# Two recurrent sequence blocks on one core: the same operations, issued in another order

## The chip, the core and the metric

The kernel runs on one core of a Trainium2 chip. Its engines work side by side, each through its own list of instructions in order: TensorE (PE, with its weight loads as PEld), VectorE (DVE), ScalarE (ACT), GpSimd (POOL), and SyncE (SP), which here only issues DMAs. The metric is the device time of one execution in microseconds (us).

## The reference

Two blocks of 2048 steps by 640 channels are computed, and their outputs stand side by side.

```python
# A: complex diagonal recurrence of 640 states, then back to real channels
Bu = einsum("bld,pd->blp", x, B_bar)
h = Lam_bar * h + Bu[:, t]            # for each t of 2048
y = 2 * einsum("blp,dp->bld", hs, C).real + x * Dskip
# B: 4-tap causal convolution of k, times v, then a 2048-long causal convolution, times q
kv = sum_t(shift(k, t) * shift_k[:, t]) * v
out = q * (irfft(rfft(kv) * rfft(ssm_k)) + kv * ssm_D)
```

## The kernel before

All of SBUF is one tile named `arena`, cut into named regions, all of PSUM one tile named `acc` of eight banks, and the only DRAM scratch is `kv_rows`. So the profile's tile names are nearly always `arena` and `acc`, and an operation is known by its line. The program builds 806 operations (`P.add`), each with a function, the cells that it reads and writes, and the engines that may run it. The string `ORDER` then lists every operation with its engine and PSUM bank: `208T0` is operation 208 on TensorE from bank 0, V is VectorE, A ScalarE, G GpSimd, S the SP queue. `emit` (line 122) walks the string and makes each operation wait for those that it depends on, by cells and by banks. The string was searched by a planner that is not in the file. A lower-case `t` is a TensorE operation of `s1` in its narrow form: 32 matmuls on 64x64 quarters of the array (line 874) in place of 16 on 128x64 halves (line 869).

Part A cuts the 2048 steps into 128 segments of 16.
- **Start.** Three parameter loads (line 355) feed one small transpose on TensorE (363), and from it come, on VectorE, ScalarE and GpSimd, tables of powers and angles: `rr` (line 443, the four 640-wide recurrence matrices, needed by line 587), sines for the Fourier steps (g_q 337 and w_q 298 on GpSimd, then the sine on ScalarE, 341 and 303), exponentials (line 375) and `al_s` (line 401, a sine). `warm` (524) runs matmuls on zeros while TensorE has nothing else. `turn_B` (509) transposes the first 128 rows of B, evicted at line 511.
- **Up.** `up2` (matmuls 566, evicted at 583), `up1` and `up0` (566 and 587, evicted at 607 and 632) compute the inputs of each step and fold them pairwise.
- **Coarse scan.** `coarse` joins the 128 segments, in two halves, on VectorE, with a swap of real and imaginary rows on TensorE (658) between; its first product with PSUM is line 661, its scan 666.
- **Down and out.** `down` spreads the states (689 and 691). If VectorE evicts, it adds the old value (709); if ScalarE does (707), TensorE adds it by another matmul (689). `project` multiplies with C: twenty matmuls of 320 columns (739) for each of 16 row sets, evicted at 748 or at 746 with an addition at 754. Row set 13 comes last, in halves (728, 730).

Part B runs in two halves of 320 channels.
- `conv` (833 to 834, with the taps' products at 205 on VectorE or 206 on ScalarE) does the 4-tap convolution for five blocks of 128 channels. k has one buffer, so the load of the next block's k (807) waits for the last tap of the one before. The rows go to `kv_rows` and come back in another layout (850).
- The long convolution is a Fourier transform in two matmul stages, `s1` (869 or 874, evicted at 879) and `s2` (893, evicted at 906), a complex product (917 to 924) and two stages back, `r2` (938, 943) and `r1` (959, with the product with q at 977, 975, 982), then a store (993). The filter goes through `s1` and `s2` as well.

Four tile shapes of the TensorE array are used: 128x128 (warm, swap, down, project), 128x64 (up, wide s1, s2), 64x64 (narrow s1, C's scaling at 556, r1) and 64x128 (r2).

Of the kernel before, what the change touches and what calls it, by code (L numbers as in the profile page):

```python
# [1084 lines left out]
def plain_order(P):  # L1085
# [16 lines left out]


ORDER = (
# [38 lines left out]
)  # L1143


# [68 lines left out]
```

## Time and profile before

| | us |
|---|---|
| median of 3 runs (194.35 to 196.14) | 195.28 |
| the profiled execution | 193.72 |
| its span, first to last instruction | 192.0 |
| TensorE busy | 182.3 |
| VectorE busy | 160.9 |
| ScalarE busy | 143.6 |
| GpSimd busy | 71.4 |

The page gives busy times and the chain of work that ended last; the chain in order of time says which engine the end hung on at each moment. [...]

### The profile page before, as it was taken

The page shows a single profiled execution, that of the slowest core. Times are in us where ns is not written, and L with a number is a line of the kernel's source. Part 1 is how long each engine was busy: PE and PEld are TensorE (multiplying, and loading weights), DVE is VectorE, ACT ScalarE, POOL GpSimd, SP SyncE. Part 2 cuts the span into 40 slices and gives each one's busy share as a digit, 9 for nine tenths or more (in the row PEclk, how much of TensorE's full clock was granted, in tenths as well). Part 3 has the DMA queues.
Part 4 walks back from the last instruction along what each step waited for, and adds up shares of the span by engine and source line. Part 5 has one row for each costly group of instructions (what it writes and reads, how often), then busy time and mean ns, then how long its engine had stood idle before and what let it go on. Part 6 is the DMA issues. An engine that isn't in the chain of part 4 may idle for free.

```text
span 192.0 us, 7688 instructions
## 1 busy us (share of the span) xinstructions
PE 182.3 (95%) x3417; PEld 120.6 (63%) x3417; DVE 160.9 (84%) x228; ACT 143.6 (75%) x178; POOL 71.4 (37%) x58
## 2 busy tenths in 40 slices
PE   5999998989998999988999999999999999999993
PEld 1455554455565765566756756775788777797772
DVE  1809998768989769999899999999988999896822
ACT  2446996999999988999999899976359753395310
POOL 8396999700000000003400279709362040480050
PEclk9999999999999999999999999999999999999999
DMA  4999999899999998959997699203996914646785
GB/s 93 198 194 186 153 172 143 169 155 246 203 203 189 225 201 122 212 97 107 130 158 210 180 136 174 45 3 106 202 220 108 191 48 133 141 156 155 170 197 155
DMA packets 107883, 30.17 MB, mean 157 GB/s; under 512 B 102602, under 2 KB 107210, under 8 KB 107850
## 3 DMA queue, kind: packets, MB, share of 16 engines
q1 hardware_dynamic: 107562, 29.35, 83.6%
q8 instruction: 27, 0.44, 1.0%
q10 hardware_dynamic: 288, 0.33, 0.6%
q14 instruction: 6, 0.05, 0.1%
HBM read 10.99 MB, written 7.86 MB: 98 GB/s over the span
## 4 chain that ended last, share of the span: by engine, by line
PE 60%; ACT 21%; DVE 13%; issue 3%; DMA 1%; SPq 0%; POOL 0%; DVEq 0%; ACTq 0%; POOLq 0%
PE acc L739 20%; PE acc L566 12%; ACT arena L879 7%; PE acc L893 6%; PE acc L938 6%; DVE arena L709 3%; PE acc L959 3%; DVE arena L906 3%; PE acc L587 3%; DVE arena L833 3%; ACT arena L206 2%; ACT arena L906 2%; PE acc L524 2%; ACT arena L341 2%; PE acc L691 2%
## 5 line engine op out<-in xcount | busy, mean ns | idle before, releaser
L566 PE MATMUL acc<-arena 128*64 128x512 bf16 x400 | 47.5, 389 | 1.1 <-ACT arena L607 0.6
L739 PE MATMUL acc<-arena 128*128 128x320 bf16 x300 | 43.0, 300 | 0.1
L906 ACT CAST arena<-acc 128x960 bf16<-128x960 f32 (+1 forms) x36 | 32.3, 923 | 7.6 <-PE acc L893 7.3
L566 PEld LDWEIGHTS <-arena 128*64 128x64 bf16 x400 | 23.4, 108 | 21.6 <-DVE arena L409 1.0
L739 PEld LDWEIGHTS <-arena 128*128 128x128 bf16 x300 | 28.4, 98 | 11.9 <-ACT arena L879 0.2
L879 ACT CAST arena<-acc 128x1024 bf16<-128x1024 f32 x36 | 34.5, 1051 | 0.6 <-PE acc L874 0.6
L893 PE MATMUL acc<-arena 128*64 128x160 bf16 x512 | 23.4, 235 | 1.5 <-ACT arena L906 0.6
L833 POOL TENSOR_TENSOR arena<-arena 128x2048 bf16<-128x2048 bf16 x1 | 4.1, 4064 | 52.3 <-DVE arena L205 52.3
L893 PEld LDWEIGHTS <-arena 128*64 128x64 bf16 x512 | 17.9, 110 | 8.0 <-ACT arena L906 3.7
L833 DVE TENSOR_TENSOR arena<-arena 128x2048 bf16<-128x2048 bf16 x14 | 19.5, 1394 | 1.1 <-ACT arena L206 0.9
L920 POOL TENSOR_TENSOR arena<-arena 128x1280 bf16<-128x1280 bf16 x4 | 10.9, 2730 | 19.0 <-DMA kv_rows<-arena 15.8
L943 ACT CAST arena<-acc 128x1024 bf16<-128x1024 f32 x15 | 14.4, 1022 | 1.4 <-POOL arena L920 0.9
L709 DVE TENSOR_TENSOR arena<-acc,arena 128x1024 bf16<-128x1024 f32 (+1 forms) x13 | 13.9, 1094 | 0.1
L583 DVE CAST arena<-acc 128x1024 bf16<-128x1024 f32 x7 | 8.5, 1217 | 6.3 <-PE acc L566 6.3
L748 DVE TENSOR_TENSOR arena<-acc,arena 128x640 bf16<-128x640 f32 x10 | 8.2, 823 | 6.5 <-PE acc L739 5.5
L205 DVE TENSOR_SCALAR arena<-arena 128x2048 bf16<-128x2048 bf16 (+1 forms) x16 | 11.0, 711 | 3.0 <-DMA arena<-in_B_k_dram 2.9
L922 POOL TENSOR_TENSOR arena<-arena 128x1280 bf16<-128x1280 bf16 x3 | 8.0, 2654 | 14.4 <-DVE arena L920 14.4
L691 PE MATMUL acc<-arena 128*128 128x512 bf16 (+2 forms) x50 | 12.6, 328 | 0.1
L206 ACT ACTIVATE arena<-arena 128x2048 bf16<-128x2048 bf16 (+2 forms) x9 | 10.8, 1207 | 2.1 <-DVE arena L833 1.7
L869 PE MATMUL acc<-arena 128*64 128x128 bf16 x320 | 11.5, 221 | 0.9 <-ACT arena L560 0.4
L975 ACT CAST arena<-acc 128x640 bf16<-128x640 f32 (+1 forms) x7 | 5.4, 808 | 9.0 <-PE acc L959 9.0
L906 DVE CAST arena<-acc 128x960 bf16<-128x960 f32 (+1 forms) x10 | 10.6, 1057 | 1.4 <-ACT arena L906 0.5
(148 smaller groups left out, 320.0 us busy)
## 6 DMA issues: line engine op xcount, KB each, us to landing
out_dram<-arena SPq DMA_DIRECT2D x31, 160.0 KB, 3.1
arena<-in_B_ssm_k_dram SPq DMA_DIRECT2D x8, 320.0 KB, 5.1
kv_rows<-arena SPq DMA_DIRECT2D x5, 512.0 KB, 3.8
arena<-kv_rows SPq DMA_DIRECT2D x16, 160.0 KB, 4.0
arena<-in_A_x_dram SPq DMA_DIRECT2D x16, 160.0 KB, 3.1
arena<-in_B_q_dram SPq DMA_DIRECT2D x8, 320.0 KB, 4.5
arena<-in_A_B_re_dram ACTq DMA_DIRECT2D x1, 160.0 KB, 2.4
arena<-in_A_B_im_dram ACTq DMA_DIRECT2D x1, 160.0 KB
```

What stands on the lines that cost most here:

```text
L206: self.SM = {nc.scalar: lambda out, in_, by: nc.scalar.mul(out, in_, by), nc.vector: vm(nc.vector), nc.gpsimd: vm(nc.gpsimd)}
L566: e.matmul(o[64 * r:64 * r + 64], lhsT=self.BT[j][:, r, d, :], rhs=self.XP[:, d, 2 * q:2 * q + 2], start=(d == 0), stop=(d == 4), skip_gro ...
L691: e.matmul(B[:, o:o + 128 * k], lhsT=c.RR[:, n, j, :], rhs=A[:, j, q:q + k, 0:128], start=not by_pe, stop=True, skip_group_check=True)
L709: e.tensor_tensor(out=o, in0=b, in1=o, op=ALU.add)
L739: e.matmul(B[:, 512 * b:512 * b + 320], lhsT=lh[j], rhs=self.CT[:, j, 320 * b:320 * b + 320], start=(j == 0), stop=(j == 9))
L833: P.add(f"ca{d}_{j}", tt, lambda e: e.tensor_tensor(out=t1, in0=t1, in1=t2, op=ALU.add), outs=[t1], ins=[t1, t2])
L869: e.matmul(B[64 * b:64 * b + 64, 128 * i:128 * i + 128], lhsT=lh[i], rhs=F[:, b, :], start=True, stop=True, tile_position=(0, 64 * b))
L879: P.add(f"e1{what}{hf}_{u}", {PACT: act(1024), PDVE: dve(1024)}, lambda e, B: c.CP[e](out=out, in_=(B.rearrange("p (l n s k) -> p k s l n" ...
L893: e.matmul(B[64 * s:64 * s + 64, 512 * b + 160 * i:512 * b + 160 * i + 160], lhsT=c.W[:, k, 64 * b:64 * b + 64], rhs=self.AS[hf][:, k, 160 ...
L906: c.CP[e](out=out, in_=b.rearrange("p r (k j n) -> p r k j n", k=n, j=4) if nj > 1 else b.rearrange("p r (k x) -> p r k x", k=n))
L938: e.matmul(B[:, 512 * s + 128 * i:512 * s + 128 * i + 128], lhsT=lh[i][s][r], rhs=rh, start=(r == 0), stop=(r == 1), tile_position=(64 * s ...
L943: P.add(f"er2{hf}_{u}", {PACT: act(1024), PDVE: dve(1024)}, lambda e, B: c.CP[e](out=out, in_=B.rearrange("p (s n b) -> p b s n", s=2, n=4 ...
```

## The change

Only the string `ORDER` is replaced. All 806 operations and all buffers stay; their order, some engines, some banks and some of the narrow forms are others.

```diff
 ORDER = (
-    "83V0 58G0 148S0 85S0 0G0 12T6 21G0 30G0 24V0 108G0 119V0 143G0 15G0 16G0 106G0 149G0 17V0 86S0 5T2 8T3 7T6 22V0 84S0 88T7 89V7 "
+    "155A0 154A0 148S0 0G0 10T4 7T5 83V0 13T6 14T0 21G0 23V0 27V0 34G0 84S0 86S0 85S0 40V0 171S0 15G0 46G0 16G0 107G0 43V0 172S0 "
...
```

Counted from the two strings: 14 operations go from ScalarE to VectorE and 14 back, 3 from VectorE to GpSimd and 5 back. The narrow form of `s1` stands 17 times where it stood 20 times. The places where TensorE goes from one tile shape to another are 85 where there were 98.

The first place is ScalarE's start. A table load is not written in the kernel: the compiler puts one wherever a function follows one of the other set. Before, all exponentials (375) stood ahead of all sines:

```order
L370 ACT_TABLE_LOAD
L370 ACTIVATE arena<-arena 128x10
L375 ACTIVATE arena<-arena 128x10
L789 CAST arena<-arena 128x20
L375 ACTIVATE arena<-arena 128x10 x2
L511 COPY arena<-acc 128x640 x2
L375 ACTIVATE arena<-arena 128x10 x2
L583 CAST arena<-acc 128x2x4x128
L401 ACT_TABLE_LOAD
L401 ACTIVATE arena<-arena 128x80
```

In the changed program ScalarE has, after the same start:

```order
L511 COPY arena<-acc 128x640 x2
L280 ACT_TABLE_LOAD
L280 ACTIVATE arena<-arena 128x64
L341 ACTIVATE arena<-arena 128x32x32
L375 ACT_TABLE_LOAD
L375 ACTIVATE arena<-arena 128x10
L243 COPY arena<-arena 128x64
L375 ACTIVATE arena<-arena 128x10
L401 ACT_TABLE_LOAD
L401 ACTIVATE arena<-arena 128x80
L341 ACTIVATE arena<-arena 128x32x32
L460 ACTIVATE arena<-arena 128x1280
```

Two sines (280, 341) moved ahead of the last two exponentials, so the program holds four table loads where it held two, and the first eviction of `up2` (583) on ScalarE comes later.

The second place is VectorE while TensorE does `up2`: its evictions (583), the additions of the first convolution (833), the recurrence tables (443) and a small table for `s1` (281). Before:

```order
L443 TENSOR_TENSOR arena<-arena 128x1280
L263 TENSOR_TENSOR arena<-arena 128x4
L583 CAST arena<-acc 128x2x4x128
L281 TENSOR_TENSOR arena<-arena 128x256
L583 CAST arena<-acc 128x2x4x128
L833 TENSOR_TENSOR arena<-arena 128x2048
L583 CAST arena<-acc 128x2x4x128
L833 TENSOR_TENSOR arena<-arena 128x2048
```

Now:

```order
L281 TENSOR_TENSOR arena<-arena 128x256
L291 CAST arena<-arena 128x2
L292 TENSOR_SCALAR arena<-arena 128x2
L833 TENSOR_TENSOR arena<-arena 128x2048
L409 MEMSET arena 64x1
L583 CAST arena<-acc 128x2x4x128
L418 RECIPROCAL arena<-arena 128x10
L583 CAST arena<-acc 128x2x4x128 x2
L443 TENSOR_TENSOR arena<-arena 128x1280
L833 TENSOR_TENSOR arena<-arena 128x2048
```

Two evictions more and the first recurrence table moved between the first and the second addition of the convolution.

The third place is TensorE after row set 3 of `project`, in `s2` of the second half (893), where `down` (691) stands between its groups. Before:

```order
L893 MATMUL acc<-arena 64x160
L691 LDWEIGHTS arena
L691 MATMUL acc<-arena 128x512
L691 LDWEIGHTS arena
L691 MATMUL acc<-arena 128x512
L893 LDWEIGHTS arena
```

Now the groups of `s2` follow each other, and `down` comes behind them:

```order
L893 MATMUL acc<-arena 64x160
L893 LDWEIGHTS arena
L893 MATMUL acc<-arena 64x160
L691 LDWEIGHTS arena
L691 MATMUL acc<-arena 128x512
```

Two changes of tile shape, into `down` and back, are gone there.

74 rows, old and new, of the table ORDER are left out of this document.

## The prediction, made before the run

> **What bounds the kernel now.** I read the page's busy times first, then the windows of four stages, then the chain in order of time. The page's first part has each engine's busy time, share and instructions:
>
> ```profile
> PE 182.3 (95%) x3417; PEld 120.6 (63%) x3417; DVE 160.9 (84%) x228; ACT 143.6 (75%) x178; POOL 71.4 (37%) x58
> ```
>
> No engine is idle enough for a simple answer. The windows cut the span, from the first `up2` on, where the chain changes engine; columns are length, then busy time of PE, PEld, DVE, ACT and POOL:
>
> ```profile
> 9.66:40.27 30.61, 29.54 (x346) 16.43 (x345) 23.36 (x23) 24.46 (x25) 25.75 (x18) 1.00 1.15 169
> 40.27:68.14 27.87, 27.28 (x529) 16.98 (x529) 22.49 (x32) 26.78 (x38) 0.00 (x0) 1.00 1.08 213
> 68.14:126.14 58.00, 55.23 (x1269) 37.03 (x1267) 55.84 (x65) 55.52 (x67) 16.98 (x5) 1.00 0.86 141
> 126.14:188.94 62.80, 62.62 (x1252) 46.97 (x1248) 53.65 (x68) 33.28 (x40) 22.86 (x12) 1.00 0.64 145
> ```
>
> From 68 to 126 us VectorE (55.84 of 58.00) and ScalarE (55.52) are full; TensorE has 2.77 us without a matmul. From 126 us on TensorE has no gap to speak of (62.62 of 62.80), and that stage sets the end. The chain, start and length of each piece, says the same:
>
> ```profile
> 7.56 2.18 PE acc L524 x10
> 9.73 11.50 PE acc L566 x100
> ...
> 25.55 2.18 DVE arena L833
> 27.75 2.01 ACT arena L206
> 29.79 2.63 DVE arena L833
> 32.44 2.00 ACT arena L206
> ...
> 39.23 1.00 ACT arena L607
> ...
> 123.16 2.37 DVE arena L879 x2
> 125.57 0.64 PE acc L869 x16
> 126.20 2.82 PE acc L739 x20
> ...
> 186.18 2.73 PE acc L728 x20
> ```
>
> It goes through fillers on TensorE to 9.7, `up2` to 21, then the first convolution, back and forth between VectorE (833) and ScalarE (206), to ScalarE's eviction of `up1` (607) at 40.2; it leaves VectorE's evictions at 125.5 and stays with TensorE up to the last row set's halves (728). So I price the change in four stages, to 40.27, to 68.14, to 126.14 and to the end.
>
> **Changes of tile shape.** Twelve `s2` matmuls alone, twenty-four in a row, twenty matmuls of `project` alone and forty in a row, from the same chain:
>
> ```profile
> 92.07 0.95 PE acc L893 x24
> ...
> 147.06 0.54 PE acc L893 x12
> ...
> 157.32 2.82 PE acc L739 x20
> ...
> 160.99 5.54 PE acc L739 x40
> ```
>
> Two groups apart take 2 x 0.54 = 1.08 against 0.95, and 5.64 against 5.54: a change of shape costs 0.10 to 0.13 us of TensorE. I take 0.10. Of the 13 changes that go, ten lie between the first swap (68.14) and row set 3 (126.14), three behind it, none before. The ten lie where VectorE and ScalarE are full, and count for 0 to -1.0. The three behind it count in full: **-0.3 us**. Three `s1` fewer are narrow; a narrow group and a wide one take
>
> ```profile
> 46.34 0.38 PE acc L874 x32
> 46.71 0.57 PE acc L869 x16
> ```
>
> so that costs at most 3 x 0.19 = 0.57 us of TensorE, in the same stage, under the same cover.
>
> **To 40.27: the start.** ScalarE gets two table loads more. What one costs, and what the first convolution waited for, is in ScalarE's timeline:
>
> ```profile
> 12.16 1.01 ACT L583 CAST arena<-acc 128x1024 bf16<-128x1024 f32 x1 [3.66 <-PE acc L566]
> 13.19 1.28 ACT L401 ACT_TABLE_LOAD   x1
> 14.48 0.27 ACT L401 ACTIVATE arena<-arena 128x80 f32<-128x80 int32 x1
> ...
> 14.80 1.27 ACT L460 ACTIVATE arena<-arena 128x1280 bf16<-128x1280 int32 x1
> ...
> 16.44 1.14 ACT L341 ACTIVATE arena<-arena 128x1024 bf16<-128x1024 int32 x1
> ...
> 21.28 3.90 ACT L206 ACTIVATE arena<-arena 128x2048 bf16<-128x2048 bf16 x2 [0.23 <-DMA arena<-in_B_k_dram]
> ```
>
> The cast ended at 13.17 and the sine began at 14.48, so a load holds ScalarE 1.31 us and two hold it 2.6. Two things cover them. ScalarE sat idle 3.66 us ahead of that cast; and the convolution's first product (206) can't start before k has landed. The load of k was issued here, in SP's timeline:
>
> ```profile
> 12.56 1.83 SPq L500 DMA_TRANSPOSE arena<-in_A_B_re_dram  x1
> 14.43 2.61 SPq L807 DMA_TRANSPOSE arena<-in_B_k_dram  x1
> ...
> 36.73 2.79 SPq L807 DMA_TRANSPOSE arena<-in_B_k_dram  x1
> ```
>
> From 14.43 to 21.28 are 6.85 us. The change puts this load ahead of the one at 12.56, so k is there at about 12.6 + 6.85 = 19.4. By then ScalarE has, from about 8.3 (my estimate for the end of the two evictions of B), 2.6 of loads, two sines of 1.14 (341), one of 1.27 (460) and seven short functions like the one of 0.27, 8.0 in all; with 2 for waits on GpSimd, whose product the first long sine needs, that is 18.3. One microsecond of cover is left, and the loads cost **0**, between 0 and 2.6. Other work of ScalarE is not held: the first evictions of `up2` go to VectorE now.
>
> [...]
>
> The convolution itself is put differently. VectorE's rows ahead of and in it:
>
> ```profile
> 14.46 1.22 DVE L583 CAST arena<-acc 128x1024 bf16<-128x1024 f32 x1 [4.87 <-PE acc L566]
> ...
> 16.29 3.16 DVE L443 TENSOR_TENSOR arena<-arena 128x1280 bf16<-128x1280 bf16 x1
> ...
> 37.44 1.64 DVE L443 TENSOR_TENSOR arena<-arena 128x1280 bf16<-128x1280 bf16 x1
> ```
>
> Now the first sum (833) can start at about 23, 2.5 earlier than at 25.5; but the second stands behind three evictions (1.22 each), the last of them paced by TensorE to end near 30, and the recurrence table (443), which takes 1.64 or, beside GpSimd's products, 3.16. It starts at 32 to 33 instead of 29.8 and ends 1.2 to 2.6 later. ScalarE's last product (2.0), an eviction (1.0), a sine (1.0) and the eviction of `up1` (1.0) follow in that order: it ends at 39.3 to 41.2, against 40.23. On the other side TensorE may start earlier. Nine fillers stand ahead of the parameter transpose, eleven behind it, where it was five and fifteen; in the cold rate five took 2.32 us, in the warm one ten take 2.18 (above):
>
> ```profile
> 1.22 2.32 PE L524 MATMUL acc<-arena 128*128 128x512 bf16 x5 [1.22 <-POOL arena L520]
> ```
>
> So `up2` may begin near 8.8, if x has landed, in place of 9.73: 0 to -0.9, most of which the later wait takes back. I take **+0.2** for the stage, between -0.9 and +2.6.
>
> **To 68.14.** ScalarE has some 2 us less to do here, since a sine of 1.3 and an eviction stand earlier; TensorE had 27.87 - 27.28 = 0.59 without a matmul, so at most -0.5. A group of `s2` (0.41, half the difference of the rows of 24 and 12 being 0.41) goes ahead of the swap: +0.4. The second load of k waits for the first convolution's last product, which now ends near 37.1 to 37.8 instead of 34.4; it was issued at 36.73 anyhow, so VectorE gets it 0.4 to 1.1 later, and carries 1.8 us more (a recurrence table of 1.5 and a cast). Its reserve is the wait ahead of the first scan:
>
> ```profile
> 68.69 0.82 DVE L661 TENSOR_TENSOR arena<-acc,arena 128x640 bf16<-128x640 f32 x1 [2.86 <-PE acc L659]
> ```
>
> 1.8 + 0.8 fits in 2.86, barely. I take **0.0**, between -0.5 and +1.5.
>
> **To 126.14.** VectorE is full, so its work counts. It takes over an eviction of 1024 columns (709) and one of 960 (906) and gives back one of 640, one of 960 and one of 256; it gets a product of 640 (718) from GpSimd and a table of 192 columns (315) from the stage before:
>
> ```profile
> 98.26 0.42 DVE L709 TENSOR_TENSOR arena<-acc,arena 128x256 bf16<-128x256 f32 x1
> ...
> 112.71 0.48 DVE L718 TENSOR_TENSOR arena<-arena 128x640 bf16<-128x640 bf16 x1
> 113.11 0.82 DVE L906 CAST arena<-acc 128x640 bf16<-128x640 f32 x1
> ...
> 118.76 2.35 DVE L709 TENSOR_TENSOR arena<-acc,arena 128x1024 bf16<-128x1024 f32 x2
> ```
>
> That is 1.18 - 0.82 - 0.42 + 0.48 = +0.42 (the two of 960 cancel), and something under 0.42 for the table. ScalarE's work is the same. VectorE's waits are only 2.2 us here, so I take **+0.5**, between -1.0 (the ten shape changes, if TensorE decides after all) and +0.8.
>
> **To the end.** TensorE alone: -0.3 from above. VectorE has about 1.5 us more (two evictions from ScalarE, products from GpSimd), in 62.80 us of which it used 53.65. The last row set's halves and its store stand as before; the load for row set 12 now waits behind three stores of part B, but its addition is done before TensorE's last group. I take -0.3, between -0.3 and +0.7.
>
> **Sum.** 0.2 + 0.0 + 0.5 - 0.3 = +0.4. The profiled execution took 193.72 (span 192.0 and 1.7 around it), 1.56 under the median; 194.1 there is **195.7** at the median of 195.28. A measurement of this kernel can tell about 1%, 1.95 us, from no change.
>
> **The rivals.**
> 1. *The start comes late (slower).* ScalarE's stream, with the loads, reaches the convolution's first product after k has landed; from there every microsecond is passed on, since the second sum, the last product and the eviction of `up1` form one chain, and a late end also delays the second k. It decides once ScalarE is more than 1.1 us later than my 18.3. For it speaks that the loads stand between products that GpSimd must make first; against it that ScalarE idled 3.66. The full price of two loads is 2.6: 195.28 + 2.6 = 197.9.
> 2. *The scan comes late (slower).* VectorE eats its reserve of 2.86 ahead of the first scan. With the second k 1.1 later and the third, which waits for the second's taps, as late again, it would be 2.2 behind plus 1.8 of work, 1.2 over the reserve; with the +0.4 and -0.1 of the rest that is 195.28 + 0.4 + 1.6 = 197.3, if the start is on its late side as well.
> 3. *TensorE decides throughout (faster).* Then all 13 changes of shape count, -1.3, and the earlier start of `up2`, -0.9: 193.1. For it speak 182.3 of busy time; against it 2.77 us without a matmul from 68 to 126.
> [...]
>
> **How the numbers follow.** My sum 0.45, the first rival 0.20, the second 0.11, the third 0.20, the fourth 0.04. The sum stays within 1%. Of rival 1 nearly all is over 1% slower, of rival 2 about all, of rival 4 all: slower 0.35. Of rival 3 all: faster 0.20. The range goes from 192.9 (rival 3 with 0.2 to spare) to 199.3 (a late start of 2.6 with my other terms and 1.2 of a late scan, 195.7 - 0.2 + 2.6 + 1.2), which holds the first three and leaves rival 4 out. The forecast's own range is 194.3 to 197.0.
>
> **What would show it.** Four table loads of 1.28 on ScalarE, each with neighbours 1.3 apart, and the first 206 waiting for k's DMA and not for ScalarE: the start is as I have it. `up1` (the matmuls behind 607 at 40.2) starting after 42 is rival 1. A wait of line 661 for TensorE that is gone is rival 2. The first row-set group after the last wide `s1` (126.14) moves by about +0.7, and from there to the last group it takes 0.3 less than 62.8. If that stage takes longer, VectorE's added work is not covered, and my last term is wrong.

## The result: 1% faster, and the profile after

| | before | after |
|---|---|---|
| median of 15 runs, us | 195.45 (194.35 to 196.83) | 193.55 (193.03 to 194.98) |
| the profiled execution, us | 193.72 | 193.30 |
| profiled execution against the median | 1.7 under | 0.25 under |

The ratio is 0.9904, with a 95% interval of 0.9877 to 0.9932: 1.9 us less. I had forecast 195.7. The medians here and below are of all runs, while the ratios are of averages that leave out the few single runs over 1.5% above the fastest of their kernel, so a ratio need not be the quotient of two medians. The last line of the table matters most for what follows: the order before varies more from run to run, and its profiled execution was faster than each of the 15; the profile after shows a usual one.

The busy times of the page after, and its windows at the places that answer to those of before (length, then busy time of PE, PEld, DVE, ACT, POOL):

```profile
PE 178.7 (93%) x3428; PEld 120.9 (63%) x3432; DVE 158.7 (83%) x231; ACT 144.6 (76%) x180; POOL 65.4 (34%) x55
```

```profile
8.90:40.43 31.53, 29.52 (x328) 17.47 (x330) 18.56 (x25) 25.68 (x28) 26.52 (x23) 1.00 1.13 170
40.43:68.06 27.63, 27.22 (x563) 17.46 (x560) 25.79 (x34) 25.48 (x39) 0.00 (x0) 1.00 1.14 186
68.06:125.38 57.32, 52.54 (x1266) 36.42 (x1268) 55.44 (x66) 54.62 (x68) 17.16 (x5) 1.00 0.95 159
125.38:188.39 63.01, 62.52 (x1257) 46.83 (x1248) 53.89 (x68) 34.92 (x41) 16.53 (x9) 1.00 0.64 145
```

One of the four places differs from before: the record of the swap's first matmul (658) is missing from this trace, so its second (659, at 68.06) stands for it. It was at 68.37 before, where the two stages beside it are:

```profile
40.27:68.37 28.10, 27.51 (x530) 17.09 (x530) 22.49 (x32) 26.90 (x39) 0.00 (x0) 1.00 1.08 213
68.37:126.14 57.77, 55.00 (x1267) 36.92 (x1265) 55.84 (x65) 55.40 (x67) 16.98 (x5) 1.00 0.86 140
```

The first stage begins 0.76 earlier than before and ends 0.16 later. TensorE's own rows say why it is no shorter in this execution:

```profile
1.00 3.68 PE L524 MATMUL acc<-arena 128*128 128x512 bf16 x9 [1.00 <-POOL arena L520]
4.62 0.17 PE L363 MATMUL acc<-arena 128*128 128x30 bf16 x1
4.65 1.46 PE L524 MATMUL acc<-arena 128*128 128x512 bf16 x6
...
8.90 2.45 PE L566 MATMUL acc<-arena 128*64 128x512 bf16 x20 [0.56 <-DMA arena<-in_A_x_dram]
12.59 1.11 PE L566 MATMUL acc<-arena 128*64 128x512 bf16 x8 [1.24 <-DMA arena<-in_A_B_im_dram]
```

`up2` starts at 8.90, as soon as x is there, and its second group waits 1.24 us for rows of B. (The view ends inside that group, so its row counts 8 matmuls of 20.) I call the start of this second group S2. It is the better mark: until then TensorE is at its fillers or waits for data, and from then on it has work. In this pair of executions S2 is 0.62 later after than before.

The starts of a few groups, taken from the profiles, divide the rest. "Up A" runs from S2 to the last group of `up1` (the one at 40.27 before), "up B" from there to the last full group of `up0` (the 566 at 65.33 before, 64.62 after), "middle" to the eviction of row set 3, "tail" to the last eviction:

| profile | S2 | up A | up B | middle | tail | time |
|---|---|---|---|---|---|---|
| before | 11.97 | 28.30 | 25.06 | 64.23 | 59.38 | 193.72 |
| after | 12.59 | 27.84 | 24.19 | 64.36 | 59.41 | 193.30 |

From S2 to the last eviction are 176.97 us before and 175.80 after, 1.17 less: the two stretches of the up groups lose 0.46 and 0.87, the middle and the tail, cut at an eviction of VectorE, gain 0.13 and 0.03.

TensorE's waits in these two stretches, before:

```profile
33.59 4.72 PE L566 MATMUL acc<-arena 128*64 128x512 bf16 x40 [0.49 <-DVE arena L409]
...
40.27 1.10 PE L566 MATMUL acc<-arena 128*64 128x512 bf16 x8 [0.59 <-ACT arena L607]
...
60.80 0.61 PE L893 MATMUL acc<-arena 128*64 128x160 bf16 x12 [0.43 <-ACT arena L906]
61.24 0.50 PE L587 MATMUL acc<-arena 128*64 128x128 bf16 x12
61.90 0.97 PE L587 MATMUL acc<-arena 128*64 128x128 bf16 x28 [0.16 <-ACT arena L632]
```

and after:

```profile
39.32 0.71 PE L874 MATMUL acc<-arena 64*64 64x64 bf16 x64 [0.77 <-DVE arena L802]
...
64.18 0.61 PE L893 MATMUL acc<-arena 128*64 128x160 bf16 x12 [0.26 <-ACT arena L906]
```

In up A the waits fall from 1.08 to 0.77, in up B from 0.59 to 0.26. That is 0.64 of the 1.33; the other 0.69 is groups that stand closer to each other, mostly (0.54) in up B. Part of it belongs to the waits: without one, a group starts before the record of the last has ended (at 38.15 before, where the rows 33.59 and 4.72 give an end at 38.31), so two waits less are worth some 0.3 more, by my estimate. And 0.19 only changed places: one `s1` group of up B is narrow where it was wide, and one of up A the other way.

One number of the text ahead of the run was wrong, the count of narrow `s1` groups. The page's rows, before and after:

```profile
L869 PE MATMUL acc<-arena 128*64 128x128 bf16 x320 | 11.5, 221 | 0.9 <-ACT arena L560 0.4 <-ACT arena L879 0.3
L874 PE MATMUL acc<-arena 64*64 64x64 bf16 x640 | 8.3, 195 | 0.5 <-ACT arena L879 0.3
```

```profile
L869 PE MATMUL acc<-arena 128*64 128x128 bf16 x304 | 11.3, 221 | 1.4 <-ACT arena L879 0.7 <-ACT arena L632 0.3 <-DVE arena L560 0.3
L874 PE MATMUL acc<-arena 64*64 64x64 bf16 x672 | 8.3, 195 | 1.0 <-DVE arena L802 0.8 <-ACT arena L879 0.2
```

640 and 672 matmuls at 32 a group are 20 and 21: there is one narrow group more, not three fewer, and TensorE gains 0.19 by it instead of losing up to 0.57. The 13 changes of shape are right, but by the traces nine of them, not ten, lie between the swap and row set 3, three behind it and one ahead.

### The profile page after: what moved, and what is told of

Its sections match the earlier page's. It is cut to its first block, busy times and chain, and to the rows that moved or that the text cites. A ratio compares the mean times of both kernels' runs of the same rounds, so it can differ in the third digit from the quotient of the medians.

```text
span 191.4 us, 7718 instructions
## 1 busy us (share of the span) xinstructions
PE 178.7 (93%) x3428; PEld 120.9 (63%) x3432; DVE 158.7 (83%) x231; ACT 144.6 (76%) x180; POOL 65.4 (34%) x55
## 4 chain that ended last, share of the span: by engine, by line
PE 46%; SPq 17%; ACT 17%; DVE 8%; DMA 6%; issue 4%; POOL 0%; ACTq 0%; DVEq 0%; POOLq 0%
PE acc L739 19%; ACT arena L879 8%; PE acc L566 6%; SPq L532 6%; PE acc L938 6%; SPq L800 5%; PE acc L893 5%; SPq L500 4%; DMA arena<-in_B_ssm_k_dram 4%; ACT arena L906 3%; PE acc L959 3%; DMA arena<-in_A_Dskip_dram 2%; PE acc L587 2%; DVE arena L709 2%; PE acc L728 1%
## 5 line engine op out<-in xcount | busy, mean ns | idle before, releaser
L566 PEld LDWEIGHTS <-arena 128*64 128x64 bf16 x400 | 24.3, 108 | 20.9 <-issue 1.7
L893 PE MATMUL acc<-arena 128*64 128x160 bf16 x512 | 22.6, 235 | 1.0 <-DVE arena L748 0.4
L893 PEld LDWEIGHTS <-arena 128*64 128x64 bf16 x512 | 18.0, 109 | 5.4 <-ACT arena L906 1.8
L833 DVE TENSOR_TENSOR arena<-arena 128x2048 bf16<-128x2048 bf16 x14 | 18.8, 1341 | 0.1
L920 POOL TENSOR_TENSOR arena<-arena 128x1280 bf16<-128x1280 bf16 x4 | 10.8, 2707 | 17.1 <-PE acc L739 15.4
L583 DVE CAST arena<-acc 128x1024 bf16<-128x1024 f32 x6 | 7.3, 1223 | 10.5 <-PE acc L566 10.5
L709 DVE TENSOR_TENSOR arena<-acc,arena 128x1024 bf16<-128x1024 f32 (+1 forms) x13 | 14.7, 1155 | 0.1
L754 POOL TENSOR_TENSOR arena<-arena 128x640 bf16<-128x640 f32 x4 | 5.6, 1426 | 24.2 <-ACT arena L746 24.2
L205 DVE TENSOR_SCALAR arena<-arena 128x2048 bf16<-128x2048 bf16 (+1 forms) x17 | 11.8, 713 | 0.1
L869 PEld LDWEIGHTS <-arena 128*64 128x64 bf16 x304 | 9.0, 109 | 3.5 <-ACT arena L879 1.3
L938 PE MATMUL acc<-arena 64*128 64x128 bf16 x320 | 11.3, 224 | 0.0
L938 PEld LDWEIGHTS <-arena 64*128 64x128 bf16 x320 | 10.5, 144 | 1.1 <-issue 0.8
```

Of the source, the lines that this page charges most:

```text
L205: vm = lambda e: lambda out, in_, by: e.tensor_scalar_mul(out=out, in0=in_, scalar1=by)
L566: e.matmul(o[64 * r:64 * r + 64], lhsT=self.BT[j][:, r, d, :], rhs=self.XP[:, d, 2 * q:2 * q + 2], start=(d == 0), stop=(d == 4), skip_gro ...
L709: e.tensor_tensor(out=o, in0=b, in1=o, op=ALU.add)
L833: P.add(f"ca{d}_{j}", tt, lambda e: e.tensor_tensor(out=t1, in0=t1, in1=t2, op=ALU.add), outs=[t1], ins=[t1, t2])
L869: e.matmul(B[64 * b:64 * b + 64, 128 * i:128 * i + 128], lhsT=lh[i], rhs=F[:, b, :], start=True, stop=True, tile_position=(0, 64 * b))
L893: e.matmul(B[64 * s:64 * s + 64, 512 * b + 160 * i:512 * b + 160 * i + 160], lhsT=c.W[:, k, 64 * b:64 * b + 64], rhs=self.AS[hf][:, k, 160 ...
```

## The experiments

All kernels hold the same 806 operations in another `ORDER`. In the diffs, which are shortened, `before` and `after` are the two lists of operations. Each ratio is to the order before as it ran in the same session; its median there was 195.45 to 195.55. The profiles have S2, up A and up B as above.

**Where in the program is the gain? Cuts.** The first kernel is the order before once more, as a measure of what two builds of one thing differ by.

```diff
-ORDER = after
+ORDER = before
```

> The unchanged order once more, as a null: every theory expects a ratio of 1.00, within 0.3%. Its profile is a second execution of the order before: the first profiled one took 193.72, 1.7 under the median of its runs. If that one was lucky at the start (theory 'start': the order before is open to late transposed loads, the changed one less), this profile is 1 to 2 us longer and has lost it before 62 us, at waits for DMAs. If the difference sits behind 126 us, 'tail' is right instead.

195.05 us at the median, ratio 0.9994 (0.9959 to 1.0029). Its profile took 194.33, 0.6 longer than the first one and not 1 to 2, and 0.56 of it lies ahead of S2 (12.53).

```diff
-ORDER = before
+ORDER = after[:267] + [x for x in before if x not in after[:267]]
```

> The changed order's first 267 operations (all that starts before some 62 us), then the order before for the rest. Theory 'start' (the gain is made in the first 62 us by the earlier up2 and the other order of loads): ratio 0.990 like the whole change. Theory 'middle' (fewer changes of tile shape between the first swap and row set 3, 10 x 0.10 us): 1.000. Theory 'tail' (three changes of shape after row set 3): 1.000.

193.45, ratio 0.9895 (0.9857 to 0.9933): the whole gain.

```diff
-ORDER = after
+ORDER = before[:267] + [x for x in after if x not in before[:267]]
```

> The mirror: the order before for its first 267 operations, the changed order for the rest. 'Start': 1.000. 'Middle': 0.990 to 0.993. 'Tail': 0.998.

196.15, ratio 1.0035 (1.0007 to 1.0064): nothing of the gain, and a little lost.

```diff
-ORDER = before
+ORDER = after[:488] + [x for x in before if x not in after[:488]]
```

> The changed order's first 488 operations (up to the second row set, some 110 us), then the order before. 'Start': 0.990. 'Middle': 0.991 to 0.994, since most of the ten changes of shape are in it. 'Tail': 1.000. Against h1_first this prices the operations 268 to 488 alone.

193.47, ratio 0.9898 (0.9859 to 0.9936), as with 267. So the changes of tile shape between 68 and 126 us and the three behind bring nothing that can be seen; what is gained is gained by operations that start ahead of 62 us.

**What in the start? Fillers and path.** Next to each other, TensorE's start before and in h2_rest, which has the same first 267 operations:

```profile
4.32 0.18 PE L363 MATMUL acc<-arena 128*128 128x30 bf16 x1 [0.79 <-DMA arena<-in_A_Lambda_re_dram]
4.35 1.44 PE L524 MATMUL acc<-arena 128*128 128x512 bf16 x3
...
7.39 2.34 PE L524 MATMUL acc<-arena 128*128 128x512 bf16 x10
9.66 4.08 PE L566 MATMUL acc<-arena 128*64 128x512 bf16 x34
```

```profile
4.28 0.18 PE L363 MATMUL acc<-arena 128*128 128x30 bf16 x1 [0.75 <-DMA arena<-in_A_Lambda_re_dram]
4.30 1.44 PE L524 MATMUL acc<-arena 128*128 128x512 bf16 x3
...
7.46 3.41 PE L524 MATMUL acc<-arena 128*128 128x512 bf16 x10
10.80 2.90 PE L566 MATMUL acc<-arena 128*64 128x512 bf16 x24
```

The parameters come at the same time, and `up2` still starts 1.14 later: ten fillers take 3.41 instead of 2.34. (The last row of each is cut off by the view.) A filler takes 0.43 us from start to start at first and 0.22 later. With five fillers ahead of the parameter transpose and a wait of 0.64 to 1.85 us behind them, the step from the one rate to the other came between about 7 and 9.6 us in seven profiles; with nine ahead and a wait of under 0.7 us or none, between 3.9 and 7.0 in eleven. The granted clock (the 1.00 near the end of this row of before) reads full from the start, so what these traces show is how far apart the fillers stand, and not why:

```profile
0.00:3.00 3.00, 1.78 (x5) 0.59 (x5) 0.60 (x5) 1.28 (x1) 2.23 (x15) 1.00 0.42 90
```

Among kernels with the same fillers the step moves by up to 3 us, and no run shows what sets it.

```diff
 TensorE's first operations
-warm11 warm4 warm7 warm6 t_par warm2 warm12 turn_B warm1 turn_B warm0 warm9 warm13 warm3 warm10 warm5 warm8
+warm9 warm6 warm12 warm13 warm3 warm5 warm8 t_par warm2 warm0 warm4 turn_B turn_B warm7 warm10 warm1 warm11
```

That is f1_fill, on the order before:

> The order before, with one thing of the order after: TensorE's first seventeen operations (fillers, parameter transpose, turn_B) stand as they do after, nine filler matmuls ahead of the transpose in place of five. Theory 'cold start': before, TensorE stops for the parameters after five fillers, stays at the slow rate (0.43 us between fillers) until 7.3 to 9.5, begins up2 at 9.7 to 10.8, and every microsecond of that reaches the end; with nine ahead the rate changes at 4 to 7 us, up2 begins by 9.6 in every execution, and the second up2 group at 12 to 12.7 with B's rows. Then the median is 193.8 to 194.5, 1.0 to 1.6 under before, and the runs lie closer together. Theory 'middle': the gain is made behind 12 us, by moved products and evictions; then this stays at 195.0 to 195.5.

194.98, ratio 0.9979 (0.9950 to 1.0009). `up2` did start at 8.95 and S2 was 11.73 in the profile, but the median gains only 0.5, with an interval that includes no gain, and the runs lie as far apart as before (193.69 to 196.68): the slow start is at most a part. The same exchange the other way, on the order after:

> The order after, with TensorE's first seventeen operations as they stood before (five filler matmuls ahead of the parameter transpose, fifteen behind). Theory 'cold start': up2 begins at 9.7 to 11.5 again; what lies over about 10.3 is passed on, since up to there the wait for B's rows (to about 12.5) takes it; the median is 194.1 to 194.9, and the runs lie further apart than after's. Theory 'middle': 193.5, as after.

194.37, ratio 0.9942 (0.9912 to 0.9972): 0.7 of the 1.9 is lost, 1.1 stays. `up2` started at 10.88, S2 was 13.17, and from S2 to the last eviction are 175.8, as in after.

```diff
-ORDER = before
+ORDER = after[:209] + [x for x in before if x not in after[:209]]
```

> The first 209 operations of the order after (to up1_8, some 40 us), then all others in the order before; the half-gain kernel took 267. In the profiled executions 0.7 us were won between 40 and 65 us (TensorE's two waits of 0.43 and 0.59 us there are gone), the rest ahead of 40. Theory 'cold start': what is won ahead of 40 stays, so 193.9 to 194.4. If the stretch from 40 to 65 made the gain: 194.9 or more. If it made none: 193.5.

193.67, ratio 0.9920 (0.9890 to 0.9950): between the expected 193.5 and 193.9. Up A is 27.84 in its profile, as in after; up B is 24.96, as before.

**Are the two table loads really free?**

```diff
 on the order after
-... 93A0 153V0 159A5 157A2 ... 38A0 ... 69A0 ... 94A0 20A0 96A0 115A0
+... 93A0 94A0 96A0 153V0 159A5 157A2 ... 38A0 ... 69A0 ... 20A0 115A0
```

> The order after with the two late exponentials moved ahead of the first sine on ScalarE: two table loads of 1.28 us are left in place of four. My prediction costed the two extra loads at nothing, since ScalarE waits for k's load at 18.3 anyhow: then this is 193.3 to 193.7, as after, with ScalarE idle longer ahead of its first product. If the loads do cost: 191 to 192.5.

193.29, ratio 0.9903 (0.9867 to 0.9938), the same as after. ScalarE's rows in after, with the loads, and then in this kernel, with two of them gone:

```profile
8.07 1.28 ACT L280 ACT_TABLE_LOAD   x1
9.37 0.35 ACT L280 ACTIVATE arena<-arena 128x64 f32<-128x64 int32 x1
11.21 1.15 ACT L341 ACTIVATE arena<-arena 128x1024 bf16<-128x1024 int32 x1 [1.49 <-POOL arena L337]
12.36 1.28 ACT L375 ACT_TABLE_LOAD   x1
13.65 0.21 ACT L375 ACTIVATE arena<-arena 128x10 f32<-128x10 f32 x1
...
14.12 1.28 ACT L401 ACT_TABLE_LOAD   x1
15.41 0.27 ACT L401 ACTIVATE arena<-arena 128x80 f32<-128x80 int32 x1
...
18.57 2.00 ACT L206 ACTIVATE arena<-arena 128x2048 bf16<-128x2048 bf16 x1 [0.24 <-DMA arena<-in_B_k_dram]
```

```profile
15.61 1.27 ACT L460 ACTIVATE arena<-arena 128x1280 bf16<-128x1280 int32 x1 [0.97 <-POOL arena L456]
...
18.43 2.00 ACT L206 ACTIVATE arena<-arena 128x2048 bf16<-128x2048 bf16 x1 [1.10 <-DMA arena<-in_B_k_dram]
```

The time saved turns into waits, 0.97 for GpSimd and 1.10 for k instead of 0.24; the first product starts at the same moment.

**Do the loads carry it?** Fillers alone had brought too little, 209 operations nearly all. Four kernels on what lies between:

```diff
-ORDER = before
+ORDER = after[:92] + [x for x in before if x not in after[:92]]
```

> The first 92 operations of the order after (all that is issued up to the first up2 group, some 9 us: fillers, parameter, x, B and first k loads, the first small operations of VectorE and GpSimd), then all others in the order before. 209 operations gave 193.67, the fillers alone 194.98. If the gain is made ahead of the first up2 (fillers and loads together): 193.6 to 194.1. If it is made by what VectorE, ScalarE and TensorE do between 9 and 40 us (order of the up groups, evictions, first convolution): 194.8 to 195.2, as with the fillers alone.

194.66, ratio 0.9948 (0.9925 to 0.9971): between the two expectations.

```diff
 SP's first 26 loads, on the order before (g3_sp); with the fillers as well (g1_fillsp)
-... ld_B1 ld_B1 ld_x4 ld_x5 ld_B2 ld_k0 ld_B2 ld_x3 ld_x2 ld_h0 ld_D ...
+... ld_B1 ld_B1 ld_x5 ld_x4 ld_k0 ld_B2 ld_B2 ld_D ld_h0 ld_x2 ld_x3 ...
```

> The order before with the fillers as after and also SP's first 26 loads as after (the first k load ahead of the second B part, 18.3 us of landing in place of 21.1; other order within each pair). Theory 'loads': in the order before a late landing of k or of B's second part holds ScalarE's and TensorE's chain in many executions, and with both parts mended the median is 193.6 to 194.2 and the runs lie within 1 us. Theory 'only the cold start': no different from the fillers alone, 194.8 to 195.2.

194.41, ratio 0.9944 (0.9922 to 0.9966): again between the two.

> The order before with only SP's first 26 loads as after; the fillers as before. Theory 'loads': half of the gain or more is here, 194.0 to 194.8. Theory 'cold start' (up2 begins at 9.7 to 11.5 whatever the loads): 195.0 to 195.6.

196.10, ratio 1.0029 (0.9999 to 1.0059), slower than either theory had it. So the loads alone bring nothing, and both theories on them, each by itself, were too simple.

> One more profile of the order before with after's fillers, whose profiled execution (193.69) was its fastest while its median was 194.98. If this one is slower, it shows where the 1.3 us of a usual execution lie: ahead of the second up2 group (start later than 12.0), between it and up1_8 (more than 28.3 us apart), or behind 40 us.

194.40, with S2 at 12.29 and up A of 28.31: between this and the faster profile of the same kernel lies S2, and nothing behind it until 65 us. Then the exchange of SP's loads on the order after, alone and with the fillers:

```diff
 SP's first 26 loads, on the order after (g5_aftersp); with the fillers as before as well (g6_path)
-... ld_B1 ld_B1 ld_x5 ld_x4 ld_k0 ld_B2 ld_B2 ld_D ld_h0 ld_x2 ld_x3 ...
+... ld_B1 ld_B1 ld_x4 ld_x5 ld_B2 ld_k0 ld_B2 ld_x3 ld_x2 ld_h0 ld_D ...
```

> The order after with SP's first 26 loads as they stood before (k's first load behind the second B part again, landing some 2.7 us later, near 21). In the profiles the second up2 group starts at 11.7 to 13.2, and from there to up1_8 all kernels with the early order before take 28.3 us, all with the order after 27.85, whatever the start. Theory 'order of the up groups and evictions': the 0.45 us stay won, and this is 193.4 to 193.9. Theory 'early k': ScalarE's first convolution product waits till 21, and the first convolution with up1_8 behind it comes 0.5 to 2 us later: 194.0 to 195.5.

195.17, ratio 0.9970 (0.9941 to 0.9998): 'early k' was right. ScalarE's rows and TensorE's in this kernel:

```profile
21.81 2.00 ACT L206 ACTIVATE arena<-arena 128x2048 bf16<-128x2048 bf16 x1 [3.21 <-DMA arena<-in_B_k_dram]
23.72 0.99 ACT L583 CAST arena<-acc 128x1024 bf16<-128x1024 f32 x1
```

```profile
24.77 2.45 PE L566 MATMUL acc<-arena 128*64 128x512 bf16 x20 [0.68 <-ACT arena L583]
27.67 2.68 PE L566 MATMUL acc<-arena 128*64 128x512 bf16 x22 [0.45 <-DVE arena L583]
```

The order after puts evictions of `up2` (583) behind products and sums that need k. With k's load late ScalarE waits 3.21, the eviction behind it is late, its banks stay full, and TensorE waits 0.68 and 0.45: up A is 29.40 instead of 27.84. Before, two evictions stood ahead of that product.

> The order after with both the fillers and SP's first 26 loads as before: what is left of the change is the order on TensorE, VectorE, ScalarE and GpSimd behind the first up2 group. If the gain is the sum of an earlier start (0.5 to 0.8) and a path shorter by 1.1 us between the second up2 group and the last eviction, this keeps the 1.1: 194.2 to 194.8. If the early loads of k are needed for it: 195 or more.

194.98, ratio 0.9964 (0.9935 to 0.9993); up A was 28.65, with 0.44 and 0.74 of waits.

> One more profile of the unchanged order. From the second up2 group's start to the end all kernels with the order before took 181.7 to 182.5. So the time of this execution, less 182.0, is where that group starts (within 0.5), and it is later the later TensorE's fillers change to their fast rate.

194.03, S2 at 12.27 and 181.76 behind it: as expected, and again far under the median of the same order.

The three parts, fillers, SP's loads and the rest of the order, have now been run in all eight combinations:

| fillers | loads | rest | median, us | ratio (95% interval) |
|---|---|---|---|---|
| before | before | before | 195.5 | 1 |
| after | before | before | 194.98 | 0.9979 (0.9950 to 1.0009) |
| before | after | before | 196.10 | 1.0029 (0.9999 to 1.0059) |
| after | after | before | 194.41 | 0.9944 (0.9922 to 0.9966) |
| before | before | after | 194.98 | 0.9964 (0.9935 to 0.9993) |
| after | before | after | 195.17 | 0.9970 (0.9941 to 0.9998) |
| before | after | after | 194.37 | 0.9942 (0.9912 to 0.9972) |
| after | after | after | 193.55 | 0.9904 (0.9877 to 0.9932) |

No part alone brings more than 0.4%. The loads cost nothing or a little by themselves, and are what lets the other parts work: on the loads as after, fillers or rest bring 1.7 us each (196.10 to 194.41 and 194.37), on the loads as before 0.5 each, and both together no more.

The spread of the runs says the same. In the seven kernels that have both fillers and loads as after, k1_swap below among them, the slowest of 6 to 15 runs is 0.8 to 2.0 us over the fastest; in the eight that have one or both as before (c0_before counted apart), the slowest of 12 to 15 is 1.8 to 5.9 over it.

**Does each gap of TensorE count?** The wait of 0.77 that is left in after (39.32 above) is for the addition 802 on VectorE, which stands behind an eviction (607) for which VectorE itself waits 1.77 us. The two were exchanged, with two banks, in f4_tables:

```diff
-235V3 ... 177V0 194t2 195V2 ... 196T0 197A0
+177V0 235V3 194t0 195V0 ... 196T2 197A2
```

> The order after with two table loads less (as measured) and two neighbours on VectorE exchanged: the addition for the filter's D (2.17 us, behind which the first s1 group waits 0.77 us of TensorE) ahead of the eviction of the first up1 group, for which VectorE sits idle 1.77 us. Theory: between the second up2 group and the end every gap of TensorE counts in full, so the end comes 0.6 to 0.8 earlier, 192.5 to 192.8 at the median, and TensorE has no wait there. Rival: the evictions or the next wait take it back, 193.2 to 193.6.

192.79 (192.47 to 193.24), ratio 0.9859 (0.9827 to 0.9892). That is the lowest median of all, 0.76 under after and 0.50 under f4_tables, but these ran in other sessions, and the intervals of the ratios overlap. VectorE's rows and TensorE's in its profile:

```profile
37.05 0.54 DVE L802 TENSOR_TENSOR arena<-arena 128x80 bf16<-128x80 bf16 x1 [2.36 <-DMA arena<-in_B_ssm_k_dram]
37.27 1.36 DVE L607 CAST arena<-acc 128x1024 bf16<-128x1024 f32 x1
```

```profile
38.48 0.60 PE L587 MATMUL acc<-arena 128*64 128x512 bf16 x4
39.01 0.71 PE L874 MATMUL acc<-arena 64*64 64x64 bf16 x64
39.65 0.64 PE L869 MATMUL acc<-arena 128*64 128x128 bf16 x16
```

The wait ahead of 874 is gone, and up A is 27.52 where f4_tables has 27.88. But the profile doesn't show that the gap counts at the end. TensorE's next wait for VectorE's evictions in `project`, in f4_tables and then here:

```profile
101.54 0.60 PE L691 MATMUL acc<-arena 128*128 128x512 bf16 x2 [0.33 <-DVE arena L748]
```

```profile
101.84 0.60 PE L691 MATMUL acc<-arena 128*128 128x512 bf16 x2 [0.92 <-DVE arena L748]
```

It is 0.59 longer, in the stage where VectorE is full (busy 55.44 of 57.32 us in after). From S2 to the last eviction are 175.81 in f4_tables and 175.76 here, so the rival's mechanism (the next wait takes it back) is what this execution shows, and it took 193.24 where the profiled one of f4_tables took 193.32. It is also the slowest of its six runs; why the others are faster stays open.

## Why the prediction was wrong, by its own steps

My 195.7 is 2.15 over the median measured. The sum was made against the profiled execution, 194.1; that execution took 193.30, so the terms were 0.8 off. The other 1.3 is the step from there to the median: I added before's 1.56, where after's profile stands 0.25 under its median.

By the prediction's own four stages the pair of profiles has (the first from the span's start, the others from the mark before, in us):

| stage, up to | forecast | before | after | difference |
|---|---|---|---|---|
| last group of `up1` | +0.2 | 40.27 | 40.43 | +0.16 |
| the swap (659) | 0.0 | 28.10 | 27.63 | -0.47 |
| row set 3 | +0.5 | 57.77 | 57.32 | -0.45 |
| last eviction | -0.3 | 62.80 | 63.01 | +0.21 |

- **To 40.27 (+0.2): the step that failed.** I saw that `up2` could start 0.9 earlier and wrote that "the later wait takes back" most of it, because the chain before goes through the convolution and ends in ScalarE's eviction ahead of 40.27. The runs show that this wait is no fixed moment. In the nine profiles whose path up to 40 us is that of before (S2 from 11.73 to 13.09, h2_rest and g4_to9 among them) up A is 28.29 to 28.34. When TensorE is later, its results, the evictions and the wait of 0.59 are later by the same amount. So what S2 loses reaches the end. And the convolution did become later, as I had it, but it was no longer what TensorE waited for: the second sum began at 31.22 (forecast 32 to 33) and ScalarE's eviction (607) ended at 39.60 (forecast 39.3 to 41.2), while TensorE's wait ahead of 40 us was for the addition 802, and up A became 0.46 shorter, where I had added 0.2:

```profile
31.22 2.92 DVE L833 TENSOR_TENSOR arena<-arena 128x2048 bf16<-128x2048 bf16 x1
38.59 1.01 ACT L607 CAST arena<-acc 128x1024 bf16<-128x1024 f32 x1 [0.56 <-PE acc L587]
```

That this pair shows +0.16, near my +0.2, is luck: it is 0.62 of a later S2, which differs from execution to execution, less the 0.46.
- **The median.** That a profile 1.56 under its median is a lucky execution I used as an offset only. It should have been a question: what in this program varies by 1.5 us, and does the change touch it? Fillers and loads together do: the range of the runs shrank from 2.5 to 2.0 us (1.0 in f3_to40).
- **To 68.14 (0.0, between -0.5 and +1.5).** The stage lost 0.47 although the `s2` group (0.4) that I had rightly moved into it did come; up B alone fell by 0.87. I had bounded the gain by TensorE's time without a matmul, 0.59. More than half came from groups set closer, which that bound leaves out: the records of matmuls in a row overlap (a late filler's lasts 0.38 us before, and the next starts 0.22 after it).
- **To 126.14 (+0.5).** The 0.45 less are mostly the `s2` group that moved out (0.41), which I had not taken off here. From the last full group of `up0` to row set 3 are 60.80 before and 60.75 after, so the work that I added for VectorE did not show; VectorE was busy 55.44 in this stage, not more than the 55.84 of before. Nor did the fewer changes of shape.
- **To the end (-0.3).** +0.21. The eleven profiles with before's order in this stage take 62.78 to 62.94, the seven with after's 62.98 to 63.64. The three changes of shape should have counted in full and did not show, and this is the sign that I had named for work of VectorE that is not covered. TensorE waits for it once behind row set 3:

```profile
129.85 0.88 PE L893 MATMUL acc<-arena 128*64 128x160 bf16 x20 [0.36 <-DVE arena L748]
```

h2_rest and h3_two agree that the part of the change behind 62 us gains nothing.
- **What was right.** Four loads of 1.28, with 1.29 to 1.32 between the neighbours of the three behind the first. ScalarE was ready for the first product (206) at 18.33 (forecast 18.3) and waited for k, though only 0.24: k was there at 18.57, not at 19.4, and the cover of 1.1 was nearly used up. f4_tables shows no cost of the loads. And the scan kept 0.90 of its reserve of 2.86 (I had "barely"):

```profile
68.39 0.82 DVE L661 TENSOR_TENSOR arena<-acc,arena 128x640 bf16<-128x640 f32 x1 [0.90 <-PE acc L659]
```

- **The rivals.** A late start and a late scan did not occur. "TensorE decides throughout" had the right engine and came nearest (193.1), but not by its terms: the 1.3 from changes of shape is not there. (In the second rival, 1.6 stands where its terms, 1.2 and +0.4 and -0.1, give no more than 1.5; and the 0.41 of an `s2` group is the whole difference of the two rows, not half. Neither decided anything.) The chances also hold 0.04 for a fourth rival, slower than the range; no run shows a load that holds ScalarE for more than the 1.29 to 1.32 us above, and f4_tables shows no cost.

So where did 1.9 us come from? From S2 to the last eviction 1.17, and all profiles agree: 176.87 to 177.31 in the nine with before's path up to 40 us, 175.76 to 175.85 in the six that have after's order up to 62 us with its loads (f2_unfill, with the fillers as before, among them). That is shown. The start adds some 0.4, an uncertain figure from few profiles: S2 is 12.77 on average in the seven with five fillers ahead of the transpose, 12.40 in the eleven with nine, and taking the fillers back costs 0.7 at the median (f2_unfill). The last 0.3 or 0.4 is not seen. All three profiles of the order before (193.72, 194.03, 194.33) are 1.1 us or more under the median of all its runs (195.5), so its usual execution is in none of them. The profile of g3_sp, the same order but for SP's first loads, took 195.50 and shows how one can look: S2 at 12.95, and 182.55 behind it, where the three have 181.8. Most of that surplus lies behind the start of the last eviction, from where the 18 profiles take 4.78 to 5.52 us to the end; what makes this part vary, no run shows. Why the loads help the fillers by 0.6 us (194.98 to 194.41) without a wait of theirs in the profiles also stays open; late landings of k or B in executions without a profile would do it, and no run shows them.

## What to carry to other kernels

When the profiled execution lies well under the median of the runs, ask first what varies and whether the change touches it: an offset carried over from before to after can be larger than all terms of the sum. A wait late in a chain is cover only if its end stands still when the start moves; here it moved along and covered nothing (up A stayed at 28.29 to 28.34 us while S2 went from 11.73 to 13.09). A gap closed ahead of a stage in which another engine is full can come back there as a longer wait (0.92 us in k1_swap, 0.33 in f4_tables). Reordering an engine's queue and reordering the loads are one change: an eviction put behind work that waits for a load is only as early as that load (in g5_aftersp ScalarE waited 3.21 us for k, and TensorE then 0.68 for the eviction behind it).

## What the runs showed of the hardware

TensorE's first matmuls ran at half the later rate (0.43 against 0.22 us for 512 columns), while the granted clock reads 1.00 (0 to 3 us, before and after), and the step between them fell anywhere in some 3 us among executions with the same fillers; with five fillers and then a wait of 0.64 to 1.85 us for a DMA it came, on average, at 8.5 us (seven profiles), with nine and a shorter wait or none at 5.1 (eleven). Behind the start the program is nearly clockwork up to the last eviction: up A repeats within 0.05 us over nine profiles, and the stretch behind the last eviction's start differs by 0.74 over all 18.
